# A fused retention and MLP kernel: the second matmul of seven token blocks by one level of Strassen, with its operand sums put into the Vector engine's idle time

## The chip, the cores and the metric

One core of a Trainium2 chip. The metric is the device time of one execution in microseconds (us); a version's time is the median of its runs. The kernel before took 316.25 us (316.0 to 316.38) when the prediction was made. TensorE is called PE here, VectorE DVE, ScalarE ACT, GpSimd POOL, and SyncE's DMA queue SP.

The experiments ran in three sets on three chips (e1 to e4, e5 to e8, e9 to e12), each beside the kernel before.

## The reference

In short:

```python
def reference(q, k, v, w_in, w_out):          # q, k, v: 8 x 8 heads x 576 x 64, f32
    scores = q @ k.transpose(0, 1, 3, 2) / 8
    ret = scores * decay(head, i - j)          # gamma^(i-j) for i >= j, else 0
    x = (ret @ v).transpose(0, 2, 1, 3).reshape(4608, 512)
    h = x @ w_in                               # 512 x 2048
    return (h * np.cos(h)) @ w_out             # 2048 x 512
```

Retention ("attention" below) runs in 40 chunks of up to 128 tokens. The MLP runs in nine blocks of 512 tokens, numbered 0 to 8. All matmuls are bf16 with f32 accumulation.

## The kernel before

Operations are recorded with what they read and write and with an assumed cost. A list scheduler (`arrange`) then plays the engines forward in time and fixes the order on each engine; semaphores are derived from that order. So the order is static.

```python
# arrange(), the choice of the next operation of one engine
for op in queue[eng][:self.WINDOW[eng]]:      # pe 24, act 12, dve 12, pool 6, sp 4
    if op not in ready or ready[op] > now:
        continue
    if any(b.i is None for b in op.boxes) and not banks:
        continue                              # no PSUM bank is free
    ...
    pick = op
    break
```

Of the MLP, one unit of the first matmul gives one k-tile of `gt` (128 of the 2048 hidden columns, for 512 tokens): four matmuls of 512 columns, a sine on ACT, a multiply on DVE. The second matmul of a block is 4 token tiles x 16 k-tiles, also of 512 columns:

```python
# mlp2(j, t, fs): token tile t of block j, k-tiles fs
for f in fs:
    inst = e.matmul(
        ap(self.BK[box.i], 512, 0, 128, 0, [1, cn]), ap(gt, NF * TB, 0, 128, f * TB + 128 * t, [1, 128]),
        ap(self.WOUT, NF * DM, 0, 128, f * DM + c0, [1, cn]),
        start=(f == 0), stop=(f == NF - 1))
...
# schedule(): block j's second matmul between block j+1's first, attention for block j+2 between both
for j in range(1, NTB):
    for i in range(16):
        if not last:
            mlp.append(m1(TB * (j + 1), TB * (j + 2), i))
        mlp.append(m2(j, i // 4, i % 4))
    ...
    run(mlp, att_of(need[j + 1], need[j + 2]) if j + 2 < NTB else [])
```

POOL scales and casts q, k and v. The k and q transposes of chunks 0 to 9 are done on PE, the later ones by DMA (`BYPE = 10`). Seven buffers stage k and v (`NSTG = 7`); the attention output `XT` is kept for all 4608 tokens. PSUM, the memory in which matmuls accumulate, has five banks for all these products; the operands lie in SBUF.

## Time and profile before

| | before |
|---|---|
| time, us | 316.31 |
| PE busy | 97% of a span of 313.8 us |
| DVE, ACT, POOL busy | 49%, 56%, 37% |
| chain that ended last | 88% PE |

The lines are from the page of the kernel before: busy time, share of the span and instructions of each engine; then the chain of work that ended last, as shares of the span. L558 is the first matmul, L583 the second.

```profile
PE 303.7 (97%) x2422; PEld 164.1 (52%) x2458; DVE 152.4 (49%) x230; ACT 175.9 (56%) x306; POOL 116.7 (37%) x138
...
PE 88%; DMA 6%; issue 1%; ACT 1%; POOL 1%; SPq 1%; DVE 0%
PE bk L558 39%; PE bk L583 38%; PE sc L431 3%; PE bk L475 3%; DMA win<-in_moe_w_in_dram 2%; PE st L446 2%; DMA stg<-in_v_dram 2%; PE bk L461 2%; DMA qstg<-in_q_dram 2%; SPq L302 1%; POOL qnat L352 1%; ACT xt L515 0%; ACT cb L566 0%; PE bk L
```

A busy PE alone doesn't prove a bound by PE, for matmuls overlap in the pipe. The groups by shape and the order of time decide. First the groups of PE in the kernel before, with busy time and mean ns of one:

```profile
L583 PE MATMUL bk<-wout,gt 128*128 128x512 bf16 x545 | 136.3, 379 | 1.0 <-issue 0.3
...
L583 PE MATMUL bk<-wout,gt 128*128 128x256 bf16 x32 | 3.7, 272 | 0.0
```

The 379 and 272 ns are from a matmul's start to its end. What it costs PE is the distance to the next start. In order of time (start, length of the merged entry, engine, line, form, count):

```profile
294.75 1.03 PE L583 MATMUL bk<-wout,gt 128*128 128x512 bf16 x4
295.61 1.03 PE L558 MATMUL bk<-xt,win 128*128 128x512 bf16 x4
...
308.79 2.56 PE L583 MATMUL bk<-wout,gt 128*128 128x256 bf16 x22
```

Four 512-column matmuls start 0.86 us ahead of the next four: 216 ns each. The 22 of 256 columns take (2.56 - 0.27) / 21 = 109 ns each. Half the columns cost half the time, even with a fresh weight load for each. And PE's idle time before all its second matmuls is 1.0 us: PE streams columns nearly all the time, so the large saving to look for on PE is fewer columns.

DVE on the other hand waits. Its largest group, and then all engines in the stretch from 130 to 206 us (from the middle of block 2 to the end of block 4, with attention; columns as in the header line):

```profile
L569 DVE TENSOR_TENSOR gt<-bk,cb 128x512 bf16<-128x512 f32 x128 | 88.1, 691 | 99.2 <-ACT cb L566 95.4 <-PE sc L431 2.2 <-ACT sbd L330 0.9
```

```profile
core 0: us, PE busy (x) PEld busy (x) DVE busy (x) ACT busy (x) POOL busy (x), PEclk, DMA share, GB/s
130.00:206.00 76.00, 74.57 (x557) 37.13 (x563) 37.99 (x49) 44.70 (x77) 36.75 (x41) 1.00 1.07 214
```

DVE is idle for half of that stretch, nearly always waiting for a sine (95.4 of the 99.2 us before this group). That is the room in which the change wants to make its sums.

### The profile page before, as it was taken

The page shows a single profiled execution, that of the slowest core. Times are in us where ns is not written, and L with a number is a line of the kernel's source. Part 1 is how long each engine was busy: PE and PEld are TensorE (multiplying, and loading weights), DVE is VectorE, ACT ScalarE, POOL GpSimd, SP SyncE. Part 2 cuts the span into 40 slices and gives each one's busy share as a digit, 9 for nine tenths or more (in the row PEclk, how much of TensorE's full clock was granted, in tenths as well). Part 3 has the DMA queues.
Part 4 walks back from the last instruction along what each step waited for, and adds up shares of the span by engine and source line. Part 5 has one row for each costly group of instructions (what it writes and reads, how often), then busy time and mean ns, then how long its engine had stood idle before and what let it go on. Part 6 is the DMA issues. An engine that isn't in the chain of part 4 may idle for free.

```text
span 313.8 us, 6228 instructions
## 1 busy us (share of the span) xinstructions
PE 303.7 (97%) x2422; PEld 164.1 (52%) x2458; DVE 152.4 (49%) x230; ACT 175.9 (56%) x306; POOL 116.7 (37%) x138
## 2 busy tenths in 40 slices
PE   7999989999999999999999999999999999999996
PEld 5776445686454545444445444444444444444444
DVE  2657525776137826655455545555444444343400
ACT  5668413895248838655556555556556555544511
POOL 3860088875556545564454545144200000000000
PEclk9999999999999999999999999999999999999999
DMA  8999999999999999999998979975100100001012
GB/s 183 234 202 201 188 218 257 230 227 190 240 198 191 201 208 198 220 217 219 213 232 196 220 149 249 220 171 96 52 33 33 38 33 36 33 33 36 33 69 100
DMA packets 133116, 49.43 MB, mean 158 GB/s; under 512 B 105312, under 2 KB 128608, under 8 KB 133088
## 3 DMA queue, kind: packets, MB, share of 16 engines
q1 hardware_dynamic: 128336, 44.84, 68.9%
q0 software_dynamic: 4752, 4.19, 8.3%
q8 instruction: 20, 0.33, 0.5%
q14 instruction: 8, 0.07, 0.1%
HBM read 36.70 MB, written 9.44 MB: 147 GB/s over the span
## 4 chain that ended last, share of the span: by engine, by line
PE 88%; DMA 6%; issue 1%; ACT 1%; POOL 1%; SPq 1%; DVE 0%
PE bk L558 39%; PE bk L583 38%; PE sc L431 3%; PE bk L475 3%; DMA win<-in_moe_w_in_dram 2%; PE st L446 2%; DMA stg<-in_v_dram 2%; PE bk L461 2%; DMA qstg<-in_q_dram 2%; SPq L302 1%; POOL qnat L352 1%; ACT xt L515 0%; ACT cb L566 0%; PE bk L541 0%; POOL nat L343 0%
## 5 line engine op out<-in xcount | busy, mean ns | idle before, releaser
L569 DVE TENSOR_TENSOR gt<-bk,cb 128x512 bf16<-128x512 f32 (+2 forms) x152 | 100.1, 663 | 102.5 <-ACT cb L566 97.8
L558 PE MATMUL bk<-xt,win 128*128 128x512 bf16 (+3 forms) x651 | 138.4, 348 | 3.4 <-issue 1.7
L583 PE MATMUL bk<-wout,gt 128*128 128x512 bf16 (+1 forms) x577 | 139.8, 373 | 1.0 <-issue 0.3
L566 ACT ACTIVATE cb<-bk,cpi 128x512 bf16<-128x512 f32 (+2 forms) x152 | 100.4, 666 | 66.8 <-PE bk L558 66.0
L558 PEld LDWEIGHTS bk<-xt,win 128*128 128x128 bf16 x672 | 62.3, 98 | 58.5 <-ACT xt L515 0.8
L583 PEld LDWEIGHTS bk<-wout,gt 128*128 128x128 bf16 x592 | 56.8, 98 | 63.5
L499 DVE TENSOR_TENSOR pt<-sc,tri 128x1024 bf16<-128x1024 f32 (+1 forms) x40 | 44.6, 1114 | 27.6 <-PE sc L431 27.4
L352 POOL TENSOR_TENSOR qnat<-qstg,wt 128x512 bf16<-128x512 f32 (+1 forms) x46 | 47.5, 1051 | 24.5 <-DMA qstg<-in_q_dram 24.4
L333 POOL CAST nat<-stg 128x512 bf16<-128x512 f32 (+1 forms) x36 | 21.9, 609 | 78.0 <-DMA stg<-in_k_dram 47.7
L515 ACT ACTIVATE xt<-bk 128x512 bf16<-128x512 f32 (+1 forms) x40 | 27.7, 692 | 34.9 <-PE sc L431 33.1
L343 POOL TENSOR_TENSOR nat<-stg,wt 128x512 bf16<-128x512 f32 (+1 forms) x39 | 40.9, 1048 | 4.7 <-DMA stg<-in_v_dram 2.8
L596 ACT ACTIVATE os<-bk 128x512 f32<-128x512 f32 (+1 forms) x37 | 21.6, 585 | 27.7 <-PE bk L583 27.7
L330 ACT ACTIVATE sbd<-st 64x256 bf16<-64x256 f32 x64 | 23.6, 369 | 2.4 <-PE st L446 1.6
L431 PE MATMUL sc<-qt,kt 64*128 64x128 bf16 (+1 forms) x320 | 15.2, 214 | 0.0
L475 PE MATMUL bk<-pt,nat 128*64 128x128 bf16 (+1 forms) x320 | 15.2, 216 | 0.0
L541 PE MATMUL bk<-dum,one 128*128 128x256 bf16 x82 | 12.7, 311 | 1.4 <-DVE lv L274 1.4
L461 PEld LDWEIGHTS bk<-qt,sbd 128*128 128x128 bf16 x128 | 9.3, 98 | 6.2 <-DVE pt L499 0.2
L461 PE MATMUL bk<-qt,sbd 128*128 128x128 bf16 (+1 forms) x128 | 11.5, 213 | 0.0
L431 PEld LDWEIGHTS sc<-qt,kt 64*128 64x128 bf16 (+1 forms) x320 | 8.8, 96 | 3.5 <-issue 0.4
L541 PEld LDWEIGHTS bk<-dum,one 128*128 128x128 bf16 x82 | 8.7, 112 | 3.3 <-DVE lv L274 1.4
L475 PEld LDWEIGHTS bk<-pt,nat 128*64 128x64 bf16 (+1 forms) x320 | 9.9, 110 | 0.9 <-DVE pt L499 0.2
L446 PE MATMUL st<-nat 128*64 128x64 bf16 x256 | 10.1, 201 | 0.0
(34 smaller groups left out, 45.2 us busy)
## 6 DMA issues: line engine op xcount, KB each, us to landing
out_dram<-os SPq DMA_DIRECT2D x35, 256.0 KB, 3.6
stg<-in_k_dram SPq DMA_DIRECT2D x32, 256.0 KB, 3.8
qstg<-in_q_dram SPq DMA_DIRECT2D x16, 512.0 KB, 5.4
stg<-in_v_dram SPq DMA_DIRECT2D x32, 256.0 KB, 5.1
wout<-in_moe_w_out_dram POOLq DMA_DIRECT2D x4, 512.0 KB, 15.1
win<-in_moe_w_in_dram POOLq DMA_DIRECT2D x3, 512.0 KB, 8.5
stg<-in_k_dram SPq DMA_DIRECT2D x8, 128.0 KB, 3.4
qstg<-in_q_dram SPq DMA_DIRECT2D x8, 128.0 KB, 3.2
```

Of the source, the lines that this page charges most:

```text
L330: self.P.add(eng, lambda e: e.activation(dst, src, AF.Copy), r=r, w=w, cost=0.127 + 0.00084 * n)
L343: self.P.add(eng, lambda e: e.tensor_tensor(ap(self.NAT[na], 2 * DM, 0, n, DM, [D, H], [1, D]), ap(self.STG[st], 2 * DM, 0, n, DM, [D, H], ...
L352: self.P.add(eng, lambda e, x=x: e.tensor_tensor(ap(self.QNAT[k], 2 * DM, 0, n, x * DM, [D, H], [1, D]), ap(self.QSTG[k], 2 * DM, 0, n, x ...
L431: inst = e.matmul(ap(self.SC, 1024, 0, n, hp * 512 + c * 128, [1, n]), ap(kt, DM, 64 * hp, 64, c * 128, [1, n]), self.queries(g, 64 * hp, ...
L461: inst = e.matmul(ap(self.BK[box.i], 512, 0, 128, c * 128, [1, n]), ap(sbd, 512, 0, 128, c * 128, [1, 128]), self.queries(g, 0, 128, c), s ...
L475: inst = e.matmul(ap(self.BK[box.i], 512, 64 * hp, 64, c * 128, [1, n]), ap(na, 2 * DM, 0, n, DM + (2 * c + hp) * D, [1, D]), ap(pt, 1024, ...
L499: self.P.add("dve", lambda e: e.tensor_tensor(ap(pt, 1024, 0, n, 0, [128, 8], [h, 2], [1, h]), ap(self.SC, 1024, 0, n, 0, [128, 8], [h, 2] ...
L515: self.P.add("act", lambda e: e.activation(ap(self.XT, 4 * TOK, 0, 128, b * S + CH * r, [TOK, 4], [1, 2], [2, h]), ap(self.BK[box.i], 512, ...
L558: inst = e.matmul(ap(self.BK[box.i], 512, 0, 128, i * n, [1, n]), ap(self.WIN, 4 * DFF, 0, 128, c * DFF + 128 * f, [1, 128]), ap(self.XT, ...
L566: self.P.add("act", lambda e: e.activation(ap(cb, TB, 0, 128, 0, [1, m]), ap(self.BK[box.i], 512, 0, 128, 0, [1, m]), AF.Sin, bias=self.CP ...
L569: self.P.add("dve", lambda e: e.tensor_tensor(ap(gt, NF * TB, 0, 128, f0 * TB + lo - TB * j, [TB, len(fs)], [1, n]), ap(self.BK[box.i], 51 ...
L583: inst = e.matmul(ap(self.BK[box.i], 512, 0, 128, 0, [1, cn]), ap(gt, NF * TB, 0, 128, f * TB + 128 * t, [1, 128]), ap(self.WOUT, NF * DM, ...
```

## The change

One level of Strassen computes the product of two 2 x 2 block matrices with seven products of half-size blocks in place of eight. Here each operand is cut in two along tokens, along k and along output columns. The seven products need five sums of token operands (made for every block), five of weights (made once) and sums of the products.

- Blocks 2 to 8 use it (`FIRST = 2`). PE gets 7 x 2 x 8 = 112 matmuls of 256 columns a block, in place of 64 of 512.
- Token sums are on DVE, in four sets of three instructions a block; two of the five overwrite `gt`. The products 4 and 2, 3 and 5, 1 and 7 share a PSUM bank in pairs: the second is accumulated on the first once that has been read out. Three combinations a block are on POOL, three on DVE, four plain evictions on ACT.
- The scheduler learns two things. An operation marked `port` waits in the model while a POOL operation, or a DVE one with two SBUF inputs, holds the port that both engines share. An operation marked `lazy` is picked only if nothing else in the window is ready. Besides, an operation that overwrites what it reads now waits for the earlier readers on its own engine too.
- To make room, `XT` becomes a ring of three blocks and `NSTG` goes from 7 to 5; output buffers go from 3 to 4. `BYPE` goes from 10 to 12: two more chunks are transposed on PE instead of by DMA.

```diff
-                        pick = op
-                        break
+                        if pick is None or not op.lazy:
+                            pick = op
+                        if not pick.lazy:
+                            break
 ...
+                    if pick.port:
+                        free[eng] += max(0.0, lock - now)
+                        lock = free[eng]
 ...
+    def token_sums(self, j, u):              # k-tiles 2u, 2u+1 and 2u+8, 2u+9 of block j
 ...
+        self.P.add("dve", lambda e: e.tensor_tensor(      # s5: 1024 columns
+            ap(self.S5, HF * TB, 0, 128, f * TB, [1, 2 * TB]), ap(gt, NF * TB, 0, 128, f * TB, [1, 2 * TB]),
+            ap(gt, NF * TB, 0, 128, (f + HF) * TB, [1, 2 * TB]), ALU.add),
+            r=keys(0, 0, 1) + keys(1, 0, 1), w=[("s5", f), ("s5", f + 1)], cost=0.62, port=True, lazy=True)
 ... # s1: 512 columns; then, in place in gt, a difference of 1024 columns
+    def product(self, j, m, box, t, at, first=True):
 ...
+            for f in range(HF):              # 8 k-tiles, 256 columns
+                inst = e.matmul(
+                    ap(self.BK[box.i], 512, 0, 128, at * HB, [1, HB]),
+                    ap(lt, lsize, 0, 128, loff + f * lstep + 128 * t, [1, 128]),
+                    ap(rt, rsize, 0, 128, roff + f * rstep, [1, HB]),
+                    start=(first and f == 0 and at == 0), stop=(f == HF - 1), skip_group_check=True)
 ... # strassen(): products in the order 4, 2, 3, 5, 1, 7, 6
-        BYPE, LEAD = 10, 3
+        BYPE, LEAD = 12, 3
 ...
+            two = self.strassen(j, last) if j >= FIRST else [m2(j, i // 4, i % 4) for i in range(16)]
 ...
+                for i, f in enumerate(fs):   # k-tiles in the order 0, 8, 1, 9, ...
+                    mlp.append(m1(TB * (j + 1), TB * (j + 2), f))
 ...
+                        mlp += two[i:i + 1]
+                    if i in (9, 11, 13, 15) and j + 1 >= FIRST:
+                        mlp.append(lambda u=(i - 9) // 2, j=j: self.token_sums(j + 1, u))
```

## The prediction

> **What bounds the kernel now.** TensorE. The page shows PE busy 303.7 of 313.8 us (97%); the chain that ended last is 88% PE, 39% of the span on the first matmul's line, 38% on the second's. The granted clock is 1.0. In the trace's order of time 512-column matmuls start every 216 ns, the 256-column ones of the tail every 109 ns, although a weight load takes 98 ns: half the columns cost half the time. DVE is busy 49%, ACT 56%, POOL 37%. DMA is full until 210 us (table of stages), but PE seldom waits for it: late K loads lead attention by 58 us.
>
> **What it removes.** A block's second matmul is 64 x 216 ns = 13.82 us. Strassen makes it 7 x 16 matmuls of 256 columns, 112 x 109 ns = 12.2 us: 1.6 us saved per block, 11.3 us in seven, all on the critical path.
>
> **What it adds.**
> - PE: two more chunks are transposed on PE instead of by DMA: 16 transposes of 56 ns plus switching, about 1 us.
> - DVE: per block four sets of sums (1024, 512 and 1024 columns, bf16, SBUF). The trace has no such sum; its 1024-column bf16 copies take 0.69 us, 512 columns 0.415. The Trainium skill, "VectorE: DVE Perf Modes", perf-mode tier table, gives a bf16 SBUF tensor_tensor two elements a cycle, the rate of these copies. Estimate: 7.2 us per block, plus three 0.69 us evictions, 9.3 us. DVE does 16 us per 31 us block now, then 25 of 29.4.
> - The port: the skill, "SBUF — State Buffer", section "SBUF: two separate sides", says that a GpSimd op and a DVE op with two SBUF inputs exclude each other. The trace agrees: two casts started 0.05 us apart took 0.69 us on DVE and 1.54 on POOL (1.04 alone). POOL is busy half of the time to 200 us, so I estimate 0.25 us extra per sum, 3 us per block. DVE is then about 90% used in blocks 2 to 5, not yet the bound.
> - POOL: three 1.04 us combinations per block. ACT as before. Weight sums: 7 us once on DVE, hidden.
> - Five staging buffers instead of seven: loads lead by enough.
>
> **Critical path.** Gain 11.3, minus 1 for transposes. Multiplies queued behind sums hold PSUM banks (Strassen products hold up to two of four or five), which should stall PE 2 to 4 us in blocks 2 to 5. At the last block no first matmul is left to fill in; its products want eight k-tiles, so PE waits for the last sine and multiply (0.69 us each): 1 to 1.5 us. Net about 7.5 us.
>
> **Predicted: 308.8 us, 304.8 to 313.2.** Faster by over 2%: 0.60; within: 0.38; slower: 0.02.
>
> **What would show it.** 784 matmuls of 256 columns at 109 ns start to start; DVE busy 152 to about 225 us; sums near 0.69 and 0.415 us without POOL, stretched by up to 1 us before 210 us; the chain above 80% PE; out stores 1.6 us closer per block in the last blocks, less so in blocks 2 to 5; one PE gap of 1 to 2 us before the last block.
>
> **What would make it wrong.** Slower: sums at one element a cycle; sums stuck behind POOL; products waiting for ACT's save of their bank; staging short, so that PE waits for attention. Faster: the schedule hides all DVE waits, leaving 305.

## The result

The change takes 306.87 us (306.38 to 307.39) against 316.31: ratio 0.9702, 95% interval 0.9682 to 0.9722. The output is correct. Here and below a ratio is the mean time of one kernel's runs over that of the other's of the same rounds, so it is not quite the ratio of the quoted medians. Where two versions of different sets of runs are compared, the text takes the difference of their ratios to the kernel before, times 316.4 us.

The page of the change, the lines that answer to those above; L575 is the first matmul, L694 a Strassen product, L600 a plain second matmul:

```profile
PE 294.2 (96%) x2756; PEld 195.3 (64%) x2792; DVE 233.6 (76%) x349; ACT 176.1 (58%) x306; POOL 155.5 (51%) x159
...
PE 75%; DMA 9%; DVE 5%; SPq 3%; issue 2%; POOL 2%; ACT 1%; DVEq 0%
```

PE lost 9.5 us of busy time, and the time fell by as much. DVE, the engine that half idled, is now at 76%. The chain passes through DVE for 5% of the span only, though its PE share is lower than predicted (75%, not above 80%).

The second matmul in order of time, in the last block of the change (same columns as before):

```profile
295.80 3.66 PE L694 MATMUL bk<-wout,s 128*128 128x256 bf16 x32
299.29 3.66 PE L694 MATMUL bk<-tw,gt 128*128 128x256 bf16 x32
```

(3.66 - 0.27) / 31 = 109 ns a matmul, as in the tail of before. The Trainium skill, "TensorE: Matmul & The Clock Gate", section "Back-to-back issue gap", gives N/2.4 + 2.5 ns for N columns at full clock as the gap of isolated matmuls, which is 109 ns for 256 and 216 for 512; the trace agrees with both.

The sums, from the view of the tile `gt` in the change (least, median and greatest ns of one, then the first and last start):

```profile
L586 DVE TENSOR_TENSOR gt<-bk,cb x152: 479/679/693, 19.6 to 290.4; 128x512 bf16<-128x512 f32 x128, 128x320 bf16<-128x320 f32 x16, 128x384 bf16<-128x384 f32 x8
...
L656 DVE TENSOR_TENSOR s<-gt x28: 674/684/1761, 93.7 to 291.2; 128x1024 bf16<-128x1024 bf16 x28
L660 DVE TENSOR_TENSOR s<-gt x28: 405/416/1510, 96.8 to 291.8; 128x512 bf16<-128x512 bf16 x28
L663 DVE TENSOR_TENSOR gt<-gt x28: 673/683/2528, 98.8 to 292.1; 128x1024 bf16<-128x1024 bf16 x28
```

Undisturbed, the sums take 0.68 and 0.41 us: 512 more columns cost 0.27 us, 0.52 ns a column. The `gt` multiplies, of which one input is in PSUM, take 0.490 us for 320 columns and 0.684 for 512, 1.01 ns a column. So the sums go about twice as fast as these, as the Trainium skill's "VectorE: DVE Perf Modes" (perf-mode tier table) has it: a bf16 `tensor_tensor` at 2x in SBUF, at 1x with an operand in PSUM. But some take up to 2.5 us, while the `gt` multiplies never exceed 0.693. The stretch is the shared port: in the trace, 31 of the 84 sums are longer than undisturbed by over 0.04 us, and each of the 31 overlaps an instruction on POOL. One such case in order of time:

```profile
254.09 1.40 POOL L720 TENSOR_TENSOR sv<-sv 128x512 f32<-128x512 f32 x1 [1.81 <-ACT sv L724]
254.28 0.69 ACT L583 ACTIVATE cb<-bk,cpi 128x512 bf16<-128x512 f32 x1 [0.27 <-PE bk L575]
254.28 1.76 DVE L663 TENSOR_TENSOR gt<-gt 128x1024 bf16<-128x1024 bf16 x1
```

POOL holds the port until 255.49 us; the difference on DVE, started at 254.28, ends at 256.04, which is 0.55 us after POOL's end. A blocked instruction isn't shown as idle time, it looks like a long one. This agrees with the Trainium skill, "SBUF — State Buffer", section "SBUF: two separate sides": one holder for a whole instruction. The three groups of sums are busy for 23.5 + 18.2 + 28.9 = 70.6 us; at their undisturbed durations they would be 28 x (0.68 + 0.41 + 0.68) = 49.6. So the port costs DVE 21 us, 3.0 us a block. That is the predicted number, but as a mean: from 130 to 206 us, where the prediction meant it, 30 sums are busy for 29.1 us instead of 17.4, 4.7 us a block; after 236 us it is 1.9.

The stretch from 130 to 206 us again, now in the change:

```profile
core 0: us, PE busy (x) PEld busy (x) DVE busy (x) ACT busy (x) POOL busy (x), PEclk, DMA share, GB/s
130.00:206.00 76.00, 74.94 (x727) 50.46 (x738) 68.65 (x90) 46.84 (x81) 52.38 (x50) 1.00 1.03 213
```

DVE went from 37.99 to 68.65 of 76 us, 90%, and PE is no less busy than before. The prediction said about 90%, but its own terms, 25 us and 3 for the port in 29.4, make 95%; that the stated number was met is partly luck. The predicted stalls of 2 to 4 us in blocks 2 to 5 are not there. All that PE waited for from 113 to 236 us, which holds these blocks (us in total, times, longest):

```profile
PE bk L575 <- issue: 0.5, 3, 0.2
PE bk L575 <- ACT sv L724: 0.2, 1, 0.2
PE bk L575 <- DVE s L656: 0.2, 1, 0.2
PE bk L575 <- DVE gt L586: 0.2, 1, 0.2
```

What it waited for in the whole run, the four largest items:

```profile
PE bk L401 <- POOL qnat L364: 1.9, 2, 1.4
PE bk L559 <- DVE lv L286: 1.4, 1, 1.4
PE bk L694 <- DVE gt L586: 0.9, 1, 0.9
PE bk L575 <- issue: 0.8, 5, 0.2
```

The first two lie in the first 50 us, in the start-up. The third is the one gap that was predicted, before the last block (1 to 1.5 us predicted, 0.93 here):

```profile
287.73 1.89 PE L575 MATMUL bk<-xt,win 128*128 128x512 bf16 x8
290.55 3.67 PE L694 MATMUL bk<-wout,gt 128*128 128x256 bf16 x32 [0.93 <-DVE gt L586]
```

The last two units of the first matmul run alone, since block 7 has 14 half products for 16 units. Then PE has nothing queued until the last sine and multiply are done.

### The profile page after: what moved, and what is told of

It is laid out like the page before. It is cut to its first block, busy times and chain, and to the rows that moved or that the text cites. A ratio compares the mean times of both kernels' runs of the same rounds, so it can differ in the third digit from the quotient of the medians.

```text
span 305.5 us, 7008 instructions
## 1 busy us (share of the span) xinstructions
PE 294.2 (96%) x2756; PEld 195.3 (64%) x2792; DVE 233.6 (76%) x349; ACT 176.1 (58%) x306; POOL 155.5 (51%) x159
## 4 chain that ended last, share of the span: by engine, by line
PE 75%; DMA 9%; DVE 5%; SPq 3%; issue 2%; POOL 2%; ACT 1%; DVEq 0%
PE bk L575 33%; PE bk L694 25%; PE bk L600 6%; DMA wout<-in_moe_w_out_dram 5%; PE sc L443 3%; SPq L314 3%; PE bk L487 2%; DVE gt L586 2%; DMA qstg<-in_q_dram 2%; PE st L458 2%; DMA stg<-in_v_dram 2%; PE bk L473 2%; DVE s L656 1%; SPq L322 1%; POOL win L328 1%
## 5 line engine op out<-in xcount | busy, mean ns | idle before, releaser
L575 PE MATMUL bk<-xt,win 128*128 128x512 bf16 (+3 forms) x642 | 133.3, 347 | 3.4 <-issue 0.8
L586 DVE TENSOR_TENSOR gt<-bk,cb 128x512 bf16<-128x512 f32 (+2 forms) x152 | 97.5, 657 | 33.8 <-ACT cb L583 32.4
L575 PEld LDWEIGHTS bk<-xt,win 128*128 128x128 bf16 x672 | 62.6, 98 | 47.3 <-ACT xt L530 1.7
L720 POOL TENSOR_TENSOR sv<-sv,os 128x512 f32<-128x512 f32 x14 | 21.0, 1499 | 54.4 <-DVE gt L586 27.7
L600 PE MATMUL bk<-wout,gt 128*128 128x512 bf16 x122 | 29.6, 379 | 0.3
L663 DVE TENSOR_TENSOR gt<-gt 128x1024 bf16<-128x1024 bf16 x28 | 28.9, 1034 | 0.0
L694 PE MATMUL bk<-tw,gt 128*128 128x256 bf16 x224 | 28.6, 273 | 0.0
L694 PE MATMUL bk<-wout,gt 128*128 128x256 bf16 x224 | 27.6, 273 | 0.9 <-DVE gt L586 0.9
L694 PE MATMUL bk<-wout,s 128*128 128x256 bf16 x224 | 27.1, 273 | 0.0
L694 PEld LDWEIGHTS bk<-wout,gt 128*128 128x128 bf16 x224 | 21.4, 98 | 7.3 <-DVE gt L586 1.8
L694 PEld LDWEIGHTS bk<-tw,gt 128*128 128x128 bf16 x224 | 21.3, 98 | 7.5 <-ACT sv L724 1.3
L656 DVE TENSOR_TENSOR s<-gt 128x1024 bf16<-128x1024 bf16 x28 | 23.5, 857 | 2.2 <-PE bk L694 2.2
L694 PEld LDWEIGHTS bk<-wout,s 128*128 128x128 bf16 x224 | 21.6, 98 | 4.9
L600 PEld LDWEIGHTS bk<-wout,gt 128*128 128x128 bf16 x128 | 11.8, 98 | 13.1 <-issue 0.4
```

The source lines that it names most:

```text
L575: inst = e.matmul(ap(self.BK[box.i], 512, 0, 128, i * n, [1, n]), ap(self.WIN, 4 * DFF, 0, 128, c * DFF + 128 * f, [1, 128]), ap(self.XT, ...
L586: self.P.add("dve", lambda e: e.tensor_tensor(ap(gt, NF * TB, 0, 128, f0 * TB + lo - TB * j, [TB, len(fs)], [1, n]), ap(self.BK[box.i], 51 ...
L600: inst = e.matmul(ap(self.BK[box.i], 512, 0, 128, 0, [1, cn]), ap(gt, NF * TB, 0, 128, f * TB + 128 * t, [1, 128]), ap(self.WOUT, NF * DM, ...
L656: self.P.add("dve", lambda e: e.tensor_tensor(ap(self.S5, HF * TB, 0, 128, f * TB, [1, 2 * TB]), ap(gt, NF * TB, 0, 128, f * TB, [1, 2 * TB]),
L663: self.P.add("dve", lambda e: e.tensor_tensor(ap(gt, NF * TB, 0, 128, f * TB + HB, [HF * TB - HB, 2], [TB, 2], [1, HB]), ap(gt, NF * TB, 0 ...
L694: inst = e.matmul(ap(self.BK[box.i], 512, 0, 128, at * HB, [1, HB]), ap(lt, lsize, 0, 128, loff + f * lstep + 128 * t, [1, 128]), ap(rt, r ...
```

## The experiments

The theory, "S": multiplies queued behind sums stall PE by 2 to 4 us. The rival, "F", formed on the two traces: the sums cost PE nothing. Beyond that: what the rest of the change costs, what the scheduler's model is worth, and where the room ends. Each kernel is the change with the edit shown.

### e1: the sums of one block only (wrong result)

```diff
-                    if i in (9, 11, 13, 15) and j + 1 >= FIRST:
+                    if i in (9, 11, 13, 15) and j + 1 == FIRST:
```

> The change, with the token sums made for the first Strassen block only; the later six blocks multiply stale or raw operands, so the result is wrong on purpose. The Strassen matmuls, evictions and POOL combinations stay; DVE loses 24 of 28 sets of sums (about 60 us of DVE time with the waits for the port). Theory S (as I predicted: gt multiplies queued behind sums hold PSUM banks and stall PE by 2 to 4 us): 303 to 305 us. Theory F (the sums fill idle DVE time and cost PE nothing but the gap before the last block): 306 to 307 us, with DVE busy about 175 us and PE busy unchanged near 294 us.

Measured: 305.76 us, ratio 0.9662 (0.9649 to 0.9674): 1.3 us faster than the change. In the stretch from 130 to 206 us:

```profile
130.00:206.00 76.00, 75.21 (x728) 50.49 (x740) 44.96 (x60) 46.58 (x80) 45.41 (x49) 1.00 1.01 206
```

DVE has 24 us less to do there than in the change, and PE gains 0.3 us. So in these blocks the sums cost PE almost nothing. The trace of this run has no gap before the last block, which fits the rest (1.1 us in e9). The time lies between the two ranges, S's up to 305 and F's from 306. The traces decide: S's stalls are not there, and the run lies under F's 306 because it also escapes that gap. For the change as scheduled, theory F holds and S is wrong.

### e2: two of the three sums twice

```diff
+        for _ in range(2):
+            self.P.add("dve", ...)           # s5
+            self.P.add("dve", ...)           # s1
```

> The change, with the s5 and s1 sums of every set issued twice (same result). Adds 28 x (0.68 + 0.41) = 31 us of DVE work alone, and waits for the port on top, with no other change. Theory S: DVE is already the engine that PE waits for in blocks 2 to 5, so nearly all the added 4.4 us per block of these four shows: 318 us or more. Theory F: DVE has about 24% idle over the span, less in blocks 2 to 5, so part is absorbed: 307.5 to 313 us.

Measured: 329.06 us (326.15 to 333.0), ratio 1.0361 (1.0328 to 1.0393). The profile fell on a run of 333.0 us that is slow (over 1.5% above the fastest of this kernel), and its clock averages 0.979; fast runs: 326.15 to 329.34 us, clock 0.984 to 0.995. 31 us more DVE work cost about 21 us. By what was expected this run falls on S's side (318 us or more), not on F's (up to 313): the change's own sums fit, but there is no room left for work on this scale. What PE waited for, and the clock in the four stretches around two gaps (L695 is the product, L657 the s5 sum, L586 the multiply):

```profile
PE bk L695 <- DVE s L657: 10.1, 4, 3.9
PE bk L695 <- DVE gt L586: 3.9, 2, 2.0
```

```profile
126.00:130.00 4.00, 1.96 (x13) 0.63 (x10) 4.00 (x5) 2.03 (x4) 2.16 (x2) 1.00 0.85 216
130.00:133.60 3.60, 3.55 (x16) 2.52 (x18) 2.25 (x3) 0.70 (x2) 2.12 (x3) 0.53 1.09 166
133.60:136.50 2.90, 0.81 (x3) 0.20 (x3) 2.28 (x4) 1.27 (x2) 2.78 (x4) 1.00 0.94 153
136.50:140.00 3.50, 3.50 (x18) 2.55 (x19) 2.92 (x4) 0.18 (x1) 0.84 (x1) 0.55 1.04 264
```

DVE is busy for all of the first 4 us while PE has nothing to do for 2.04 of them, and then PE runs at half clock for some 3.4 us. So a saturated DVE is paid for twice: the wait, and the slow clock after it. The wait is the larger part: if the time at a reduced clock is lost in proportion, a mean clock of 0.984 to 0.995 costs the fast runs an estimated 2 to 5 of the 21 us. Nor are all the waits in blocks 2 to 5: 5.7 us of them (1.83 ahead of 310.65 us, 3.86 ahead of 318.18) stand before and in the last block.

### e3: the port taken out of the scheduler's model

```diff
-        op.port, op.lazy = port, lazy
+        op.port, op.lazy = False, lazy
```

> The change, with the shared port taken out of the scheduler's model only (every operation unmarked); same operations, another order. If the port's model is part of what makes the change pay: 309 us or more. If the order that it gives matters little, since DVE and POOL wait for each other by themselves and PE has other work queued: within 1 us of 306.9.

Measured: 310.36 us, ratio 0.9823 (0.9789 to 0.9858): (0.9823 - 0.9702) x 316.4 = 3.8 us slower than the change, with the same instructions. PE's largest wait:

```profile
PE bk L694 <- DVE gt L586: 2.4, 2, 1.6
```

A gap of 1.6 us stands at the first Strassen block (113.6 us), which the change doesn't have; the other wait, 0.8 us, is the gap before the last block. Of the 3.8 us, the trace thus puts 1.6 down to this gap. The model of the port is part of what makes the change pay.

### e4: sums in program order

```diff
-        op.port, op.lazy = port, lazy
+        op.port, op.lazy = port, False
```

> The change, with the sums no longer lazy in the scheduler (a ready sum goes in program order in front of multiplies and evictions that were added later). If letting sums fill idle time is what keeps PE fed: 308.5 us or more, with more wait of PE and ACT for DVE. If not: within 1 us of 306.9.

Measured: 309.62 us, ratio 0.9796 (0.9770 to 0.9823): 3.0 us slower than the change. Again PE waits 2.3 us, in three places, for multiplies ahead of products; one of them, 0.9 us, is the gap before the last block, which the change has too, so that 1.4 us are new. Letting the sums yield is worth about as much as the port. This is probably how S came to be wrong: I costed the sums' effect on multiplies as if they were queued in program order.

### e5: no Strassen block, the rest of the change kept

```diff
-        FIRST = 2
+        FIRST = 9
```

(And the tail of the last block split as in the kernel before.)

> The changed kernel with no Strassen block at all (the second matmul of every block plain, its tail split as in the kernel before); what stays is the rest of the change: two more chunks transposed on PE, five staging buffers, XT as a ring of three blocks, four output buffers, k-tiles of the first matmul in the order 0, 8, 1, 9. If the sum of the prediction is right term by term (transposes 1 us, staging and ring nothing): 317.0 to 317.6 us. Rival: the smaller staging or the ring costs time as well (319 us or more), so Strassen gives more than I counted; or the fewer DMA transposes help the start (below 316).

Measured: 316.96 us, ratio 1.0017 (1.0002 to 1.0031), 0.5 us over the kernel before. Ring, staging and the k-tile order cost nothing that shows; the reading is completed by e12.

### e6: Strassen in the last three blocks

```diff
-        FIRST = 2
+        FIRST = 6
```

> The changed kernel with Strassen in the last three blocks only. If every Strassen block gains the same 1.6 us of PE time and the gap before the last block (1.1 us) is paid once: 317.3 - 4.9 + 1.1 = 313.5 us, and the four blocks added by the full change are worth 6.5 us. If blocks with attention and POOL work gain less than the last ones, as I predicted (2 to 4 us lost in blocks 2 to 5): the difference to 306.9 is 2.5 to 4.5 us, so 309.4 to 311.4 us.

Measured: 312.90 us, ratio 0.9889 (0.9876 to 0.9903). From e5: (1.0017 - 0.9889) x 316.4 = 4.05 us for three blocks; with the gap of 1.1 us (e9) added back, 1.7 us a block. From here to the change: (0.9889 - 0.9702) x 316.4 = 5.9 us for four blocks, 1.5 us a block. The arithmetic of PE says 1.6, or 6.5 us for four, so that 0.6 us is lost in them, which is within the noise of these ratios. Blocks with attention and POOL work gain practically as much as the last ones, against my prediction.

### e7: the transposes of chunks 10 and 11 by DMA again

```diff
-        BYPE, LEAD = 12, 3
+        BYPE, LEAD = 10, 3
```

> The change with the transposes of chunks 10 and 11 put back on DMA, as before. If they only cost PE time (16 transposes of 56 ns and switching): 305.8 to 306.1 us. If DMA transposes of these chunks would come too late, in the stretch where loads limit attention: 307 us or more.

Measured: 311.08 us (309.16 to 312.43), ratio 0.9823 (0.9794 to 0.9852): 3.8 us slower than the change, although PE has less work. The two kernels, from 95 us on; first the change, then e7:

```profile
95.00:115.00 20.00, 19.84 (x185) 10.09 (x188) 18.93 (x26) 13.68 (x24) 12.87 (x13) 1.00 1.09 210
115.00:130.00 15.00, 14.68 (x132) 10.59 (x129) 12.79 (x19) 7.87 (x14) 9.38 (x10) 1.00 1.13 193
130.00:165.00 35.00, 34.58 (x339) 23.35 (x343) 31.44 (x40) 21.40 (x37) 24.91 (x24) 1.00 1.10 221
```

```profile
95.00:115.00 20.00, 17.93 (x164) 8.98 (x164) 17.66 (x23) 15.82 (x29) 11.31 (x13) 1.00 0.86 197
115.00:130.00 15.00, 13.86 (x130) 7.41 (x131) 15.00 (x23) 9.77 (x17) 9.51 (x9) 1.00 1.16 218
130.00:165.00 35.00, 33.11 (x319) 24.15 (x323) 28.68 (x39) 17.91 (x32) 24.48 (x23) 1.00 1.05 207
```

PE loses 1.9, 0.8 and 1.5 us, 4.2 in all. In the first stretch it waits most for ACT's write of an attention result; in the second DVE is busy for 15.00 of 15 us. Attention is late: the result of chunk 13 is written at 94.6 us here, at 90.4 in the change.

### e8: block 7's half products two places later (wrong result, by mistake)

```diff
+                    elif j + 2 == NTB:
+                        mlp += two[i - 2:i - 1] if i > 1 else []
```

> The change with block 7's half products moved two places later among the first-matmul units of block 8, so that one is left to run after the last of these. If the gap of 1.1 us before the last block is only PE waiting for the last sine and multiply with nothing queued: the gap shrinks to under 0.4 us and the time is 305.8 to 306.3 us. If the last block's sums are late too: the gap moves to a later product and the time stays within 0.3 us of 306.9.

Measured: 305.31 us, but wrong (relative error 0.24). The dependencies follow the order in which operations are recorded. With the products two places later, the sums of block 8 were recorded ahead of block 7's last reads of `s1`, so block 7 got some of block 8's operands. By this account, read from the code, there is no race, only another program, which a check for races would not see. That e9, with the sums recorded later, is correct agrees with it. The time is not used.

### e9: the same, mended

```diff
+                    elif j + 2 == NTB:
+                        mlp += two[i - 2:i - 1] if i > 1 else []
 ...
-                    if i in (9, 11, 13, 15) and j + 1 >= FIRST:
-                        mlp.append(lambda u=(i - 9) // 2, j=j: self.token_sums(j + 1, u))
+                    at_i = (11, 12, 13, 15) if j + 2 == NTB else (9, 11, 13, 15)
+                    if i in at_i and j + 1 >= FIRST:
+                        mlp.append(lambda u=at_i.index(i), j=j: self.token_sums(j + 1, u))
```

> The run before with products moved to the end, mended: there the sums of the last block were issued before block 7 had read s1, so they overwrote it; here the first sets come after units 11, 12, 13 and 15. If the gap before the last block was only PE with nothing queued: correct, 305.3 to 305.9 us, no gap over 0.4 us before the last block. If the later sums now hold up the last block instead: 306.5 us or more.

Measured: correct, 305.68 us (305.13 to 308.58), ratio 0.9668 (0.9634 to 0.9702). In order of time, the end of block 7 and the start of block 8:

```profile
287.39 1.03 PE L575 MATMUL bk<-xt,win 128*128 128x512 bf16 x4
288.25 1.04 PE L694 MATMUL bk<-tw,gt 128*128 128x256 bf16 x8
289.12 3.66 PE L694 MATMUL bk<-wout,gt 128*128 128x256 bf16 x32
```

A half product now stands between the last unit and the last block, and no idle time is listed before the latter. The gap is gone, and the gain of (0.9702 - 0.9668) x 316.4 = 1.1 us fits it, though the intervals of the two ratios touch. With all its sums this kernel is as fast as e1, which leaves nearly all of them out. It has the lowest median of the correct versions.

### e10: Strassen from block 1 on, with e9's order

```diff
-        FIRST = 2
+        FIRST = 1
```

> The mended order with Strassen from block 1 on, eight blocks (the kernel has the switch). If a block's gain is PE time alone: another 1.6 us, about 304 us. If block 1, in the stretch where loads limit attention and weight sums must be done earlier on DVE, can't hide its sums: 305.5 us or more, with PE gaps between 65 and 110 us.

Measured: 319.28 us, ratio 1.0084 (1.0066 to 1.0103): 13 us slower than e9 for one more block, and slower than the kernel before. The mean clock is 0.983. The stretch where it happens, and what PE waited for in it:

```profile
65.00:95.00 30.00, 24.05 (x297) 16.90 (x298) 29.75 (x40) 18.47 (x35) 23.68 (x23) 0.89 1.11 212
95.00:115.00 20.00, 15.89 (x153) 8.91 (x154) 18.95 (x26) 10.62 (x19) 14.91 (x15) 0.91 0.96 199
```

```profile
PE bk L694 <- DVE gt L586: 3.5, 1, 3.5
PE bk L473 <- DMA kt<-nat: 3.0, 1, 3.0
```

DVE is busy for 29.75 of 30 us, PE for 24, and the clock drops as in e2: a mean of 0.983 over 316.5 us is an estimated 5 of the 13 us. The weight sums, block 1's token sums and the attention that is still catching up meet here. How much of the 13 us each of the three has is not taken apart.

### e11: the transposes of chunks 12 and 13 on PE too, with e9's order

```diff
-        BYPE, LEAD = 12, 3
+        BYPE, LEAD = 14, 3
```

> The mended order with the transposes of chunks 12 and 13 on PE too. Moving those of chunks 10 and 11 to PE was worth 4 us although it adds 1 us of PE work. If attention is still what PE waits for behind chunk 12: faster than the mended order by 0.5 us or more. If the two chunks were enough, only the PE work shows: 0.8 to 1.5 us slower (16 transposes for the query pair, 8 for the keys).

Measured: 307.02 us, ratio 0.9700 (0.9682 to 0.9718), 1.0 us slower than e9. That is the expected price of the transposes on PE, but one e9 run of 308.58 us widens the intervals so far that they overlap. What is clear is that there is no gain of 0.5 us or more in sight: two chunks were probably enough.

### e12: no Strassen block, transposes by DMA

e5 with `BYPE = 10`.

> No Strassen block, and the transposes of chunks 10 and 11 on DMA as in the kernel before; left of the change are the ring, the five staging buffers, the four output buffers and the order of k-tiles. If the transposes on PE cost 1 us of PE work and late attention only hurts where DVE is full of sums: 315.9 to 316.4 us, under the 316.96 of the run without Strassen. If late attention hurts by itself in this layout: above 317.5 us, as much as 321.

Measured: 316.16 us, ratio 0.9992 (0.9975 to 1.0008). Without Strassen the two chunks' transposes on PE cost (1.0017 - 0.9992) x 316.4 = 0.8 us, though the two intervals overlap a little; they gain nothing. With Strassen the same edit gains 3.8 us (e7). The result of chunk 13 is written at 94.9 us here, as late as in e7. So late attention as such doesn't hurt here; together with the Strassen schedule it does. That attention's late DVE work collides with the weight sums and the first token sums is what e7's full DVE suggests; it was not tested by itself.

## Why the prediction was right

Predicted 308.8 (304.8 to 313.2), measured 306.87, on the predicted side of 2%. Term by term, in us:

| term | predicted | measured | by |
|---|---|---|---|
| PE columns saved, seven blocks (measured: net of stalls) | -11.3 | -11.0 | e5 to e9: (1.0017 - 0.9668) x 316.4 |
| transposes on PE, own cost | +1 | +0.8 | e12 to e5 |
| ring, staging, buffers, order | 0 | -0.3, within noise | e12 |
| stalls in blocks 2 to 5 | +2 to +4 | 0 to 0.6, inside the first row | e1, e6, e9 |
| gap before the last block | +1 to +1.5 | +1.1 | e9 |
| sum | -7.5 | -9.4 | change: (0.9702 - 1) x 316.4 |

The measured rows are differences along one chain of kernels (before, e12, e5, e9, the change), so they add up by construction; their sum tests nothing. What tests the first row is the arithmetic of columns beside it. The set-to-set differences of about 1 us carry about as much noise.

**Right, and shown.** PE was the bound, and half the columns cost half the time: 109 against 216 ns. The sums run twice as fast per column as the multiplies (0.68 and 0.41 us). The port costs 3.0 us a block of DVE time, as a mean. There is one gap before the last block, for the reason given, and giving PE something to run there removes it.

**Mis-sized: "Multiplies queued behind sums hold PSUM banks, which should stall PE 2 to 4 us in blocks 2 to 5".** This term is nearly nought, 0 to 0.6 us. Leaving out 24 of the 28 sets gives PE 0.3 us in that stretch, and e9 with all of them equals e1. The mechanism isn't imaginary: take either half of the scheduler's new knowledge away and 3 to 4 us come back (e3, e4), of which PE's waits for multiplies show about 1.5. I had read these two edits as details of the change; they are what removes the cost I charged. The prediction's own list had this case under "faster: the schedule hides all DVE waits, leaving 305", and e9 is at 305.7.

**Misjudged in kind: the transposes.** I counted them as a cost of 1 us. That cost is real, but they are in the change because the Strassen schedule can't bear late attention: without them 3.8 us are lost. I had seen in the trace of before that loads were full until 210 us, and asked only whether PE waited for them there.

**Near miss: DVE "about 90% used in blocks 2 to 5, not yet the bound".** Not the bound, and at 90%, though by the prediction's own terms it would have been 95%; over the whole run DVE is busy for 233.6 us where about 225 were predicted. The edge is close and steep. 4.4 us more DVE work a block (e2), or one Strassen block more at the wrong time (e10), cost 21 and 13 us: PE's waits, and the half clock that followed gaps of 2 to 4 us.

## What to carry to other kernels

Where PE streams columns back to back and another engine has idle time, one level of Strassen is worth what the count of columns says, an eighth of that matmul, as long as each half-width matmul still covers its weight load (here 109 ns over 98; no run has one that does not). Whether the extra sums are free is a matter of order rather than of the sum of busy times: have them yield to the work that feeds PE, and give the scheduler every exclusive resource that the trace shows. Before adding more, look at the fullest stretch of the engine that absorbs it, not at its mean; here 76% over the span was 90% in the middle, and the next step fell off the edge.

## What the Trainium skill lacked or had wrong

- "TensorE: Matmul & The Clock Gate", section "Back-to-back issue gap": it says that in a real stream of weight load and matmul pairs the spacing is about 131 ns for 512 columns, and that its isolated formula over-counts there. Here streams with a weight load for each matmul run at 216 ns for 512 columns and 109 ns for 256, which is the isolated formula.
- Same page, part 1, on the clock gate: it ties the slow clock to an idle window of about 3.4 us. In e2's profiled run PE idled for 2.04 us ahead of 130.0 us and for 2.08 us ahead of 136.5 us, and the granted clock was 0.53 and 0.55 in the 3.6 and 3.5 us after these. In e10 it idled for 2.95 us ahead of 81.3 us, and the clock was 0.50 from 81 to 84 us. Gaps of 1.97 us (ahead of 208.7 us) and 1.83 us (ahead of 310.65 us) in e2 and of 0.93 us in the change had no such effect (clock 1.00 after them). So shorter gaps than the page's window can cost half the clock; these traces don't settle where the limit lies. The same part also tells of short idle times between groups of matmuls that make the clock swing, but gives no length for them.
- "SBUF — State Buffer", section "SBUF: two separate sides": the lock is as stated. What it doesn't say is how it looks in a profile: the waiting instruction has no idle time before it but a longer duration, 1.76 us instead of 0.68 for a 1024-column sum. Summed over the sums of the change that is 21 us of DVE time that counts as busy.
